# A spectral mixer with a token MLP: 256-column products with one weight tile paired into 512-column products

## The chip, the core and the metric

The kernel runs on one core of one Trainium2 chip, in one launch. The metric is the device time of that launch in microseconds. The matrix engine (TensorE, PE in the profile) multiplies tiles into PSUM, eight banks of 512 float32 columns by 128 partitions; VectorE (DVE) and ScalarE (ACT) read PSUM and work in SBUF; GpSimd (POOL) and SyncE (SP) mostly issue DMAs here. Each engine has its own queue of instructions, and semaphores order work between them.

## The reference

What matters of it (S = 2048 tokens, D = 512 channels, F = 1792 hidden units; all float32):

```python
x = A_x
xn = _layernorm(x, axis=-1)
# A: global filter
X = rfft2(xn) * (w_r + 1j * w_i)
s = irfft2(X)
# B: token mixing
h = _layernorm(xn)
u = gelu(einsum("bsd,sf->bdf", h, w1) + b1)
y = einsum("bdf,fs->bds", u, w2) + b2
g = silu(y.transpose(0, 2, 1))
return x + s * g
```

The change lies in the second product of B, here GEMM2: 2048 tokens by 512 channels, summed over 1792 hidden units.

## The kernel before, in words

Stages up to about 212 us: layer norms and GEMM1 with GELU, the spectral filter between them, and the forms of the hidden activations described below. The last stage is GEMM2 with the inverse channel transform and the output. Only it is touched.

**One step of Strassen's method (Winograd's form).** GEMM2 is cut into 2 x 2 blocks: output tokens (tile j0 = p and tile j1 = p + 8), hidden units (two halves of seven tiles of 128) and channels (left and right 256). Seven products of sums of blocks replace eight. Each product n has a weight form (seven 128 x 128 tiles, `w2_form`) and an activation form (seven tiles of 128 x 256, `forms`).

**High and low parts.** Each operand is split into a high part, rounded to a short mantissa, and a low remainder, and a product is three matrix products: high weight with high activation, high weight with low activation, low weight with high activation. A form tile holds the high part in its first 256 columns and the low part in the next 256, side by side (`high_low`, `form_parts`). For weights, ACT writes the high part (L706) and DVE the low part (L707).

**The loop.** `for p in range(NP)` runs over eight pairs of output tiles; inside, `ORDER = (1, 2, 5, 6, 3, 7, 4)` runs over the products. Each has 7 form tiles x 3 = 21 products of 256 columns (L828). They accumulate in the left halves of three banks: `bx` (bank 2 or 3, alternating with p) takes 1, then 6, 7 and 4 on top; `by` (bank 4) takes 2; `bz` (bank 5) takes 5, then 3 on top. As soon as a sum stands, ACT copies it out (`copied`, L790: p1, p5, v2), or DVE adds an earlier copy to it (`summed`, L798: c11, c12, c22), and ACT puts the result through SiLU (`gate`, L794). `finish` (L802) multiplies by the spectral result on DVE and a DMA on POOL's queue adds it to the output (L804), where x already lies.

**What else runs in a pair.** `channels` (L763) does the inverse channel transform of one output tile, and its DVE operations (L767 to L779) give y, which is split into ch (ACT) and cl (DVE, both L143); `spectral` (L146 to L148) then does three 512-column products, called the rotations below. DVE adds weight blocks for the forms 6 and 3 (L720, L726). SP's queue loads weight blocks (L695), and POOL's queue adds a second block in the DMA (L697). The weight forms are in three buffers (tag w2f) and are made two products ahead.

**What sets the order.** The code states the work of the stage in program order, and a scheduler places the instructions on each engine; each engine then runs its own in that order. So operations of one step can stand between those of another.

Of the kernel before, what the change touches and what calls it, by code (L numbers as in the profile page):

```python
# [8 lines left out]
F32 = mybir.dt.float32  # L9
# [6 lines left out]
P = 128  # L16
S, D, F = 2048, 512, 1792
# [3 lines left out]
NH = NF // 2  # L21
# [113 lines left out]
def spectral_mixer_kernel(tc, x, w1, b1, w2, b2, wk, we, wx, c_f, c_ft, c_d, c_i, c_g, c_h, out):  # L135
    nc = tc.nc
    V, A, G, T, SY = nc.vector, nc.scalar, nc.gpsimd, nc.tensor, nc.sync

    def pool(stack, side, name, bufs):
        return stack.enter_context(tc.tile_pool(name=name, bufs=bufs, side=side, reuse_waits="tile"))  # L140
# [9 lines left out]
    with tc.tile_pool(name="ps", bufs=1, space=PSUM) as psp, ExitStack() as left, ExitStack() as right:  # L150
        ps = psp.tile([P, 8, 512], F32, name="ps")
# [180 lines left out]

        def form_parts(n, i):
            t, k = form[i][n]
            return t[:, k, :D // 2], t[:, k, D // 2:]


        BATCHES = ((((4, 2), (10, 2)), (7, 2, 0, 1)), (((6, 1), (12, 2)), (7, 0, 1)))
# [45 lines left out]
        m = moments("m0", 2)  # L384
# [3 lines left out]
        m = {k: t[:, :1] for k, t in m.items()}  # L388
# [12 lines left out]
        c = turned(0, m, 0)  # L401
# [4 lines left out]
        m = moments("m2", 2)  # L406
        of.update({2: (m, 0), 3: (m, 1)})
        folds = iter(())
        for j in range(NJ):
            more = j + 1 < NJ  # L410
# [33 lines left out]
            if more:  # L444
# [7 lines left out]
                c = turned(j + 1, *of[j + 1])  # L452
# [4 lines left out]
            if more:  # L457
                low(w[1][1], raws[j + 1, 1], w[1][0])
                if FIRST <= j < FIRST + NE:
                    i = j - FIRST  # L460
# [5 lines left out]
                if j % 2 == 0 and j + 4 < NJ:  # L466
                    m = moments(f"m{j + 4}", 2)
# [23 lines left out]
        T = Kept(T, keep)  # L491
# [184 lines left out]
        for n in range(8):  # L676
            a, b, c, d, e, f = PACE[n]
# [69 lines left out]
        fp = pool(left, "left", "fin", 1)  # L747
# [6 lines left out]
        def gathered(j):  # L754
            yt = fp.tile([P, 4, P], F32, name=f"yt{j}", tag="yt", bufs=2)
            A.activation(yt.rearrange("p b (l c) -> p b l c", c=2), ey[:, :, :, j], AF.Copy)
            return yt

        def channels(j, yt):

            pe = ps[:, 6 + j // NP].rearrange("p (h b c) -> p h b c", b=2, c=P)
            for b in range(4):
                T.matmul(pe[:, b % 2, b // 2], yt[:, b], ci[:, b], start=True, stop=True)  # L763
# [15 lines left out]
            V.scalar_tensor_tensor(yv[:, 1, :, 1], t, -RT, ev[:, :, 1], op0=ALU.mult, op1=ALU.add)  # L779
            ch = fp.tile([P, D], F32R, name=f"ch{j}", tag="ch", bufs=2)  # L780
            cl = fp.tile([P, D], F32R, name=f"cl{j}", tag="cl", bufs=2)
            split(ch, cl, y)
            return ch, cl

        def spectral(j, y):
            mm3(ps[:, j // NP], cft[:, 0], cft[:, 1], *y, True, True)

        def copied(name, src):
            t = fp.tile([P, HD], F32, name=name, tag=name.split("_")[0])
            A.activation(t, src, AF.Copy)  # L790
            return t

        def gate(g, j, cols, src, scale):
            A.activation(g[:, cols], src, AF.Silu, bias=b2t[:, j:j + 1], scale=scale)  # L794

        def summed(name, a, b):
            t = fp.tile([P, HD], F32, name=name, tag="c", bufs=2)
            V.tensor_add(t, a, b)  # L798
            return t

        def finish(g, j, cols):
            V.tensor_mul(g[:, cols], ps[:, j // NP, cols], g[:, cols])  # L802
            if j + 1 < NJ:
                G.dma_start(out[:, j, cols], g[:, cols], accum_op=ALU.add)  # L804
            else:
                V.tensor_add(g[:, cols], g[:, cols], xr[:, cols])
                SY.dma_start(out[:, j, cols], g[:, cols])

        left_, right_, whole = slice(0, HD), slice(HD, D), slice(0, D)
        y0 = channels(0, gathered(0))  # L810
        for p in range(NP):
            j0, j1 = p, p + NP
            g0, g1 = (fp.tile([P, D], F32, name=f"g{j}", tag="g", bufs=2) for j in (j0, j1))
            bx, by, bz = ps[:, 2 + p % 2, :HD], ps[:, 4, :HD], ps[:, 5, :HD]
            for k, n in enumerate(ORDER):
                wf = ready.pop(0)
                w = next(wforms, None)
                if w is not None:
# [5 lines left out]
                o = {1: bx, 6: bx, 7: bx, 4: bx, 2: by, 5: bz, 3: bz}[n]  # L824
                for m, i in enumerate(FORMS):
                    uh, ul = form_parts(n, i)
                    for a, (wi, ui) in enumerate(((0, uh), (0, ul), (1, uh))):
                        T.matmul(o, wf[:, wi, i], ui, start=m + a == 0 and n in (1, 2, 5), stop=m == NH - 1 and a == 2,  # L828
                                 skip_group_check=n in (6, 3, 7, 4))
                if n == 1:  # L830
                    p1 = copied(f"p1_{p}", bx)
                    spectral(j0, y0)
                elif n == 5:
                    p5 = copied(f"p5_{p}", bz)
                elif n == 2:
                    gate(g0, j0, left_, summed(f"c11_{p}", by, p1), 1.0)
                elif n == 6:
                    v2 = copied(f"v2_{p}", bx)
                    y1 = channels(j1, yt)
                elif n == 3:  # L840
                    gate(g0, j0, right_, summed(f"c12_{p}", bz, v2), 1.0)
                    finish(g0, j0, whole)
                elif n == 7:
                    gate(g1, j1, right_, summed(f"c22_{p}", bx, p5), -1.0)
                    spectral(j1, y1)
                    if p + 1 < NP:
                        y0 = channels(j0 + 1, yt)
                    else:
                        finish(g1, j1, right_)
                else:  # L850
                    gate(g1, j1, left_, bx, -1.0)
                    finish(g1, j1, whole if p + 1 < NP else left_)


# [35 lines left out]
```

## Time and profile before

| | us |
|---|---|
| median of 3 runs | 391.57 (389.78 to 392.61) |
| the profiled execution | 387.47 |
| its span, first to last instruction | 385.7 |
| GEMM2 stage, from 212.2 to the end of the span | 173.5 |
| mean granted TensorE clock | 0.993 of full speed |

Rows of the profile read: engine, line, operation, output tile <- input tiles, shapes, count. In groups the numbers behind the bar are total busy us and mean ns of one, then idle time before it and what ended it; in a timeline the first two are start and length in us. An engine's operations overlap at their ends, so the distance from one start to the next is shorter than a row's length. The chain of waits follows the last instruction back to what released each step. PE's ends are modelled; its starts carry the pace.

### The profile page before, as it was taken

To read this page: it belongs to the slowest core of one execution; us is meant where nothing else is said; L and a number is where in the kernel's file an instruction comes from. 1 tells how busy PE (TensorE), PEld (TensorE's weight loads), DVE (VectorE), ACT (ScalarE), POOL (GpSimd) and SP (SyncE) were. 2 spreads that over 40 slices of the span, in tenths; PEclk is the share of its full clock that TensorE was granted. 3 is DMA by queue.
4 is the path that set the end of the run, shared out by engine and by line. 5 is a ranking of instruction groups with operands and counts; after the bars stand their busy time and mean duration, and the time that the engine had idled before them with its cause. 6 is when DMAs were issued, how large, how long until landed. Compare 5 with 4: busy or idle time off the path is not lost.

```text
span 385.7 us, 7939 instructions
## 1 busy us (share of the span) xinstructions
PE 374.0 (97%) x2872; PEld 328.8 (85%) x2872; DVE 323.2 (84%) x734; ACT 227.6 (59%) x412; POOL 78.6 (20%) x133
## 2 busy tenths in 40 slices
PE   7999999999999999999799989999999999999994
PEld 4888888888778878777588979999999999999994
DVE  5899999986579999897995999796979787887873
ACT  4677776764843455575417695565656564646541
POOL 2133233231302333233001003030202020210100
PEclk9999999999999999999899999999999999999999
DMA  8974777312636889988828398896979787885602
GB/s 262 300 251 155 266 254 241 97 55 82 198 77 173 211 226 256 245 226 193 259 71 253 57 274 208 214 215 166 201 153 214 140 230 143 220 165 156 98 0 55
DMA packets 39143, 70.01 MB, mean 182 GB/s; under 512 B 5424, under 2 KB 21440, under 8 KB 38976
## 3 DMA queue, kind: packets, MB, share of 16 engines
q1 hardware_dynamic: 30048, 48.14, 39.8%
q0 software_dynamic: 9056, 21.38, 29.3%
q8 instruction: 22, 0.36, 0.4%
q14 instruction: 17, 0.14, 0.1%
HBM read 61.10 MB, written 8.13 MB: 179 GB/s over the span
## 4 chain that ended last, share of the span: by engine, by line
PE 73%; DVE 9%; DMA 9%; issue 5%; ACT 1%; POOL 1%; SPq 0%; DVEq 0%; POOLq 0%; ACTq 0%
PE ps L828 28%; PE ps L377 20%; PE ps L132 16%; PE ps L241 4%; PE ps L763 3%; DMA s<-in_w_dram 2%; DMA out_dram<-g 2%; DVE w2f L707 2%; DMA w1l<-in_w_dram 2%; PE ps L366 1%; DMA w1s<-in_w_dram 1%; PE ps L147 1%; PE ps L148 1%; DMA hf<-in_c_h_dram 1%; DVE xc L589 1%
## 5 line engine op out<-in xcount | busy, mean ns | idle before, releaser
L377 PE MATMUL ps<-h,w1h 128*128 128x512 f32 x224 | 58.7, 398 | 0.0
L132 PE MATMUL ps<-h,w1h 128*128 128x512 f32 x152 | 49.6, 408 | 0.0
L707 DVE TENSOR_TENSOR w2f<-s,w2f 128x896 fp32r<-128x896 f32 x32 | 34.8, 1092 | 16.6 <-ACT w2f L706 15.8
L377 PEld LDWEIGHTS ps<-h,w1h 128*128 128x128 f32 x224 | 40.9, 188 | 7.9
L828 PE MATMUL ps<-fa,w2f 128*128 128x256 f32 x336 | 43.4, 282 | 0.0
L828 PE MATMUL ps<-fc,w2f 128*128 128x256 f32 x336 | 41.7, 280 | 1.0 <-DVE w2f L707 0.6
L828 PE MATMUL ps<-fb,w2f 128*128 128x256 f32 x336 | 42.5, 281 | 0.1
L828 PEld LDWEIGHTS ps<-fa,w2f 128*128 128x128 f32 x336 | 41.6, 188 | 0.8
L828 PEld LDWEIGHTS ps<-fc,w2f 128*128 128x128 f32 x336 | 40.3, 188 | 1.6 <-DVE w2f L707 0.8
L828 PEld LDWEIGHTS ps<-fb,w2f 128*128 128x128 f32 x336 | 40.4, 188 | 0.5 <-DVE c L798 0.5
L697 POOL DMA_DIRECT2D s<-in_w_dram x16 | 13.9, 870 | 122.0 <-DMA s<-in_w_dram 36.7
L706 ACT ACTIVATE w2f<-s 128x896 fp32r<-128x896 f32 x32 | 30.2, 949 | 14.1 <-DVE s L720 10.9
L132 PEld LDWEIGHTS ps<-h,w1h 128*128 128x128 f32 x152 | 27.7, 192 | 9.9 <-issue 4.9
L707 DVE TENSOR_TENSOR w2f<-a,w2f 128x896 fp32r<-128x896 f32 x24 | 26.0, 1085 | 9.5 <-ACT w2f L706 9.5
L132 PE MATMUL ps<-h,w1l 128*128 128x512 f32 x76 | 30.1, 396 | 2.8 <-DMA w1l<-in_w_dram 2.8
L377 PE MATMUL ps<-h,w1l 128*128 128x512 f32 x112 | 30.6, 389 | 0.0
L706 ACT ACTIVATE w2f<-a 128x896 fp32r<-128x896 f32 x24 | 22.8, 950 | 11.8 <-PE ps L828 7.3
L377 PEld LDWEIGHTS ps<-h,w1l 128*128 128x128 f32 x112 | 21.0, 188 | 4.5
L589 DVE SCALAR_TENSOR_TENSOR xc<-xc,turn,px 128x512 f32<-128x512 f32 x32 | 23.9, 747 | 0.2 <-issue 0.2
L372 DVE TENSOR_TENSOR w1l<-w1r,w1h 128x512 fp32r<-128x512 f32 (+1 forms) x32 | 20.9, 652 | 2.1 <-ACT w1h L369 1.9
L804 POOL DMA_DIRECT2D out_dram<-g x15 | 13.5, 902 | 43.8 <-DVE g L802 43.8
L794 ACT ACTIVATE g<-c,b2t 128x256 f32<-128x256 f32 x24 | 12.1, 505 | 15.9 <-DVE c L798 13.3
(128 smaller groups left out, 765.5 us busy)
## 6 DMA issues: line engine op xcount, KB each, us to landing
a<-in_w_dram SPq DMA_DIRECT2D x24, 448.0 KB, 4.0
wt<-in_wk_dram POOLq DMA_DIRECT2D x16, 512.0 KB, 4.7
s<-in_w_dram SPq DMA_DIRECT2D x16, 448.0 KB, 4.3
s<-in_w_dram POOLq DMA_DIRECT2D x16, 448.0 KB, 6.7
w1s<-in_w_dram SPq DMA_DIRECT2D x36, 128.0 KB, 3.2
w1r<-in_w_dram SPq DMA_DIRECT2D x16, 256.0 KB, 3.6
xc<-px SPq DMA_DIRECT2D x64, 64.0 KB, 4.1
x<-in_x_dram SPq DMA_DIRECT2D x15, 256.0 KB, 3.7
```

What stands on the lines that cost most here:

```text
L132: return lambda *args, **kw: self.keep(operation(*args, **kw))
L241: T.matmul(z[:, b], h[:, b * P:(b + 1) * P], c, start=True, stop=True)
L372: keep(V.tensor_sub(dst, src, hi.bitcast(F32)))
L377: T.matmul(ps[:, bank + i], w[wi][:, i * P:(i + 1) * P], hj, start=first and j == 0, stop=last and j == NJ - 1)
L589: V.scalar_tensor_tensor(to, zt, turn[:, k:k + 1], px[:, ::-1], op0=ALU.mult, op1=ALU.add)
L697: G.dma_start(t, w2_half(*added), accum_op=ALU.add)
L706: A.activation(wf[:, 0], v, AF.Copy)
L707: V.tensor_sub(wf[:, 1], v, wf[:, 0].bitcast(F32))
L763: T.matmul(pe[:, b % 2, b // 2], yt[:, b], ci[:, b], start=True, stop=True)
L794: A.activation(g[:, cols], src, AF.Silu, bias=b2t[:, j:j + 1], scale=scale)
L804: G.dma_start(out[:, j, cols], g[:, cols], accum_op=ALU.add)
L828: T.matmul(o, wf[:, wi, i], ui, start=m + a == 0 and n in (1, 2, 5), stop=m == NH - 1 and a == 2, skip_group_check=n in (6, 3, 7, 4))
```

## The change

A form tile's two parts lie side by side, so that the high weight tile can meet both in one product of 512 columns: `form_parts` also returns the whole tile. The left half of the bank then sums high x high and low x high, the right half high x low. In the pairs 0 to 6 (`wide`) each form tile has one product of 512 columns and one of 256; the last pair keeps three of 256. What is read from a bank is 512 columns wide, and the two halves are added on DVE: `copied` copies both halves, `summed` adds copy and bank over 512 columns and then the right half to the left, in place. For product 4, which was read straight from PSUM by the gate, the right half is copied by ACT and added by DVE. The copies now share one tag with two buffers, p5 has its own.

```diff
         def form_parts(n, i):
             t, k = form[i][n]
-            return t[:, k, :D // 2], t[:, k, D // 2:]
+            return t[:, k], t[:, k, :D // 2], t[:, k, D // 2:]
...
         def copied(name, src):
-            t = fp.tile([P, HD], F32, name=name, tag=name.split("_")[0])
+            n = src.shape[-1]
+            five = name[:2] == "p5"
+            t = fp.tile([P, D], F32, name=name, tag="p5" if five else "part", bufs=1 if five else 2)[:, :n]
             A.activation(t, src, AF.Copy)
             return t
...
-        def summed(name, a, b):
-            t = fp.tile([P, HD], F32, name=name, tag="c", bufs=2)
-            V.tensor_add(t, a, b)
-            return t
+        def summed(src, t):
+            V.tensor_add(t, src, t)
+            if t.shape[-1] > HD:
+                V.tensor_add(t[:, :HD], t[:, :HD], t[:, HD:])
+            return t[:, :HD]
...
-            bx, by, bz = ps[:, 2 + p % 2, :HD], ps[:, 4, :HD], ps[:, 5, :HD]
+            wide = p + 1 < NP
+            bx, by, bz = (ps[:, b, :D if wide else HD] for b in (2 + p % 2, 4, 5))
...
                 for m, i in enumerate(FORMS):
-                    uh, ul = form_parts(n, i)
-                    for a, (wi, ui) in enumerate(((0, uh), (0, ul), (1, uh))):
-                        T.matmul(o, wf[:, wi, i], ui, start=m + a == 0 and n in (1, 2, 5), stop=m == NH - 1 and a == 2,
-                                 skip_group_check=n in (6, 3, 7, 4))
+                    both, uh, ul = form_parts(n, i)
+                    if wide:
+                        T.matmul(o, wf[:, 0, i], both, start=m == 0 and fresh, stop=m == NH - 1, skip_group_check=True)
+                    else:
+                        T.matmul(o, wf[:, 0, i], uh, start=m == 0 and fresh, stop=False, skip_group_check=more)
+                        T.matmul(o, wf[:, 0, i], ul, start=False, stop=False, skip_group_check=more)
+                    T.matmul(o[:, :HD], wf[:, 1, i], uh, start=False, stop=m == NH - 1, skip_group_check=more or wide)
...
-                    gate(g1, j1, left_, bx, -1.0)
+                    gate(g1, j1, left_, summed(bx[:, :HD], copied(f"low_{p}", bx[:, HD:])) if wide else bx, -1.0)
```

Where the instructions stand now. On PE, in pair 4, between the products 5 and 6 (w2f5_4, w2f6_4 are the weight forms, fc the activation forms), before:

```order
L828 MATMUL ps_58<-fc5_2766,w2f5_4_3836 128x256 x3
L828 MATMUL ps_58<-fc6_2772,w2f5_4_3836 128x256 x3
L828 MATMUL ps_58<-fc2_1437,w2f6_4_3866 128x256 x3
L828 MATMUL ps_58<-fc1_1562,w2f6_4_3866 128x256 x3
L828 MATMUL ps_58<-fc0_2421,w2f6_4_3866 128x256 x3
```

and after:

```order
L833 MATMUL ps_58<-fc5_2766,w2f5_4_3652 128x512
L837 MATMUL ps_58<-fc5_2766,w2f5_4_3652 128x256
L833 MATMUL ps_58<-fc6_2772,w2f5_4_3652 128x512
L837 MATMUL ps_58<-fc6_2772,w2f5_4_3652 128x256
L833 MATMUL ps_58<-fc2_1437,w2f6_4_3675 128x512
L837 MATMUL ps_58<-fc2_1437,w2f6_4_3675 128x256
```

Three instructions of 256 columns per form tile have become one of 512 and one of 256; the order of the form tiles is the same.

On DVE, at the same place of pair 4, with the sum of product 2 (c11 before, p1 after), the weight additions (s1) and the low parts of the weight forms, before:

```order
L720 TENSOR_TENSOR s1_12_3613<-s1_12_3613,a12_4_3616 128x896
L707 TENSOR_TENSOR w2f6_4_3866<-s1_12_3613,w2f6_4_3866 128x896
L798 TENSOR_TENSOR c11_4_3897<-ps_58,p1_4_3860 128x256
L726 TENSOR_TENSOR s1_12_3613<-s1_12_3613,a11_4_3648 128x896
L707 TENSOR_TENSOR w2f3_4_3901<-s1_12_3613,w2f3_4_3901 128x896
L707 TENSOR_TENSOR w2f7_4_3929<-s4_4_3676,w2f7_4_3929 128x896
```

and after:

```order
L720 TENSOR_TENSOR s1_12_3468<-s1_12_3468,a12_4_3471 128x896
L799 TENSOR_TENSOR p1_4_3669<-ps_58,p1_4_3669 128x512
L801 TENSOR_TENSOR p1_4_3669<-p1_4_3669 128x256
L707 TENSOR_TENSOR w2f6_4_3675<-s1_12_3468,w2f6_4_3675 128x896
L726 TENSOR_TENSOR s1_12_3468<-s1_12_3468,a11_4_3496 128x896
L707 TENSOR_TENSOR w2f3_4_3703<-s1_12_3468,w2f3_4_3703 128x896
L707 TENSOR_TENSOR w2f7_4_3724<-s4_4_3517,w2f7_4_3724 128x896
```

The sum of product 2 has moved ahead of the low part of form 6, and the addition of the halves (L801) stands behind it.

On DVE, later in pair 4, around the sum of product 7 (p5) and the output tile g4, after:

```order
L801 TENSOR_TENSOR v2_4_3744<-v2_4_3744 128x256
L799 TENSOR_TENSOR p5_4_3722<-ps_58,p5_4_3722 128x512
L767 TENSOR_TENSOR es5_3822<-ps_58,od5_3820 128x256
L805 TENSOR_TENSOR g4_3650<-ps_58,g4_3650 128x512
L801 TENSOR_TENSOR p5_4_3722<-p5_4_3722 128x256
L768 TENSOR_TENSOR es5_3822<-ps_58,od5_3820 128x256
L707 TENSOR_TENSOR w2f2_5_3837<-a11_5_3706,w2f2_5_3837 128x896
```

Before, the multiplication (L802) of that tile came first, then the sum of product 7, then the low part of form 2 and both halves of es. Now the halves of v2 stand ahead of the sum of product 7, and the multiplication, whose gate needs them, two operations behind.

On PE, from the end of product 7 to product 4 of pair 4, after:

```order
L837 MATMUL ps_58<-fb6_2771,w2f7_4_3724 128x256
L146 MATMUL ps_58<-ch12_3763,cft_63 128x512
L763 MATMUL ps_58<-cd_64,yt5_3772 128x128 x4
L833 MATMUL ps_58<-fd2_1366,w2f1_5_3793 128x512
L147 MATMUL ps_58<-cl12_3764,cft_63 128x512
L148 MATMUL ps_58<-ch12_3763,cft_63 128x512
L837 MATMUL ps_58<-fd2_1366,w2f1_5_3793 128x256
L833 MATMUL ps_58<-fd2_1366,w2f1_5_3793 128x512
L837 MATMUL ps_58<-fd2_1366,w2f1_5_3793 128x256
L833 MATMUL ps_58<-fb2_1436,w2f4_4_3767 128x512
```

Before, only the rotations (L146 to L148) and the four products of L763 stood between the products 7 and 4, and product 1 of the next pair followed product 4. Now two couples of that product 1 (w2f1_5) stand ahead of product 4 as well.

More of the change, by code (lines that the diff above doesn't have):

```diff
@@ L824, in spectral_mixer_kernel @@
                 o = {1: bx, 6: bx, 7: bx, 4: bx, 2: by, 5: bz, 3: bz}[n]
+                fresh, more = n in (1, 2, 5), n in (6, 3, 7, 4)
                 for m, i in enumerate(FORMS):
-                    uh, ul = form_parts(n, i)
-                    for a, (wi, ui) in enumerate(((0, uh), (0, ul), (1, uh))):
-                        T.matmul(o, wf[:, wi, i], ui, start=m + a == 0 and n in (1, 2, 5), stop=m == NH - 1 and a == 2,
-                                 skip_group_check=n in (6, 3, 7, 4))
+                    both, uh, ul = form_parts(n, i)
[5 more added lines that the diff above has]
+                    T.matmul(o[:, :HD], wf[:, 1, i], uh, start=False, stop=m == NH - 1, skip_group_check=more or wide)
                 if n == 1:
@@ L835, in spectral_mixer_kernel @@
                 elif n == 2:
-                    gate(g0, j0, left_, summed(f"c11_{p}", by, p1), 1.0)
+                    gate(g0, j0, left_, summed(by, p1), 1.0)
                 elif n == 6:
@@ L840, in spectral_mixer_kernel @@
                 elif n == 3:
-                    gate(g0, j0, right_, summed(f"c12_{p}", bz, v2), 1.0)
+                    gate(g0, j0, right_, summed(bz, v2), 1.0)
                     finish(g0, j0, whole)
                 elif n == 7:
-                    gate(g1, j1, right_, summed(f"c22_{p}", bx, p5), -1.0)
+                    gate(g1, j1, right_, summed(bx, p5), -1.0)
                     spectral(j1, y1)
```

## The prediction

> **What bounds the kernel now.** I read the page first: busy time, then the chain of work that ended last.
>
> ```profile
> PE 374.0 (97%) x2872; PEld 328.8 (85%) x2872; DVE 323.2 (84%) x734; ACT 227.6 (59%) x412; POOL 78.6 (20%) x133
> PE 73%; DVE 9%; DMA 9%; issue 5%; ACT 1%; POOL 1%; SPq 0%; DVEq 0%; POOLq 0%; ACTq 0%
> PE ps L828 28%; PE ps L377 20%; PE ps L132 16%; PE ps L241 4%; PE ps L763 3%; DMA s<-in_w_dram 2%; DMA out_dram<-g 2%; DVE w2f L707 2%; DMA w1l<-in_w_dram 2%; PE ps L366 1%; DMA w1s<-in_w_dram 1%; PE ps L147 1%; PE ps L148 1%; DMA hf<-in_c_h_dram 1%; DVE xc L589 1%
> ```
>
> TensorE (PE) holds the chain, and the changed line, L828, is its largest single part, 28% of the span. Since L828 runs only in the last stage (212 us to the end), I asked for that chain in order of time, and for the busy time of two whole pairs (one round of the loop over p).
>
> ```profile
> 302.11 7.42 PE ps L828 x63
> 322.63 7.42 PE ps L828 x63
> 343.34 7.42 PE ps L828 x63
> ...
> 302.11:322.63 20.52, 20.52 (x172) 20.12 (x171) 16.73 (x33) 12.20 (x20) 3.47 (x4) 1.00 0.81 183
> 322.63:343.34 20.71, 20.71 (x171) 20.30 (x171) 16.90 (x33) 12.18 (x20) 3.47 (x4) 1.00 0.82 181
> ```
>
> A pair lasts (343.34 - 302.11) / 2 = 20.62 us. The windows give length and then busy time of PE, its weight loads, VectorE (DVE), ScalarE (ACT), GpSimd: PE is busy through both, DVE for 16.8 us, ACT for 12.2, at the full granted clock. So in a settled pair PE sets the pace, and DVE has 3.8 us to spare. Where that lies is in DVE's timeline (in brackets: idle time before, and what ended it):
>
> ```profile
> 322.59 1.09 DVE L720 TENSOR_TENSOR s<-s,a 128x896 f32<-128x896 f32 x1
> 324.76 1.09 DVE L707 TENSOR_TENSOR w2f<-s,w2f 128x896 fp32r<-128x896 f32 x1 [1.08 <-ACT w2f L706]
> 325.77 0.42 DVE L798 TENSOR_TENSOR c<-ps,p 128x256 f32<-128x256 f32 x1
> 326.10 1.08 DVE L726 TENSOR_TENSOR s<-s,a 128x896 f32<-128x896 f32 x1
> 328.28 2.21 DVE L707 TENSOR_TENSOR w2f<-s,w2f 128x896 fp32r<-128x896 f32 x2 [1.10 <-ACT w2f L706]
> 331.34 1.09 DVE L707 TENSOR_TENSOR w2f<-a,w2f 128x896 fp32r<-128x896 f32 x1 [0.85 <-ACT w2f L706]
> 340.72 0.69 DVE L802 TENSOR_TENSOR g<-ps,g 128x512 f32<-128x512 f32 x1 [0.55 <-ACT g L794]
> ```
>
> Two holes, 1.08 and 1.10 us, are a relay: DVE adds a weight form (L720, L726), ACT rounds its high part, DVE takes the low part (L707). They don't shrink when PE is faster. The other two, 0.85 and 0.55, come from ACT operations that had themselves waited for PE, and give way.
>
> The first two pairs look otherwise:
>
> ```profile
> 215.00:220.00 5.00, 4.93 (x42) 4.72 (x41) 5.00 (x12) 3.39 (x7) 0.00 (x0) 1.00 0.01 2
> 220.00:225.00 5.00, 4.09 (x34) 3.69 (x33) 4.32 (x9) 4.22 (x8) 0.00 (x0) 1.00 0.75 247
> 225.00:230.00 5.00, 4.37 (x35) 4.05 (x34) 4.90 (x12) 5.00 (x9) 0.87 (x1) 1.00 0.89 229
> 230.00:235.00 5.00, 5.00 (x42) 4.86 (x41) 5.00 (x14) 3.43 (x6) 0.31 (x1) 1.00 0.90 307
> ...
> 222.20 0.51 PE L828 MATMUL ps<-fc,w2f 128*128 128x256 f32 x2 [0.29 <-ACT w2f L706]
> 223.33 2.50 PE L828 MATMUL ps<-fc,w2f 128*128 128x256 f32 x19 [0.62 <-DVE w2f L707]
> 227.61 0.50 PE L146 MATMUL ps<-ch,cft 128*128 128x512 f32 x1 [0.63 <-ACT ch L143]
> ```
>
> From 215 to 235 us DVE is busy 19.2 of 20, and PE waits for DVE and ACT: there PE is not the bound.
>
> **The change, part by part.** *The products.* A couple of 256-column products with one weight tile becomes a 512-column one. What each costs is its distance to the next start in a dense stretch:
>
> ```profile
> 204.69 0.40 PE L146 MATMUL ps<-h,w1h 128*128 128x512 f32 x1
> ...
> 211.97 0.39 PE L148 MATMUL ps<-h,w1l 128*128 128x512 f32 x1
> 212.20 2.63 PE L828 MATMUL ps<-fd,w2f 128*128 128x256 f32 x21
> ...
> 304.42 5.11 PE L828 MATMUL ps<-fc,w2f 128*128 128x256 f32 x42
> 309.37 1.05 PE L763 MATMUL ps<-cd,yt 128*128 128x128 f32 x8
> 310.18 2.72 PE L828 MATMUL ps<-fa,w2f 128*128 128x256 f32 x21
> ```
>
> From 204.69 to 212.20 there are 33 products of 512 columns: 7.51 / 33 = 0.2276 us. Between 304.42 and 309.37 there are 42 of 256: 4.95 / 42 = 0.1179 us. A merge therefore saves 2 x 0.1179 - 0.2276 = 8.2 ns: nearly all of the time is the columns, whose number stays. There are 7 products x 7 forms = 49 merges in a pair and 7 wide pairs (the last stays narrow), 343 in all: 0.40 us a pair, 2.8 us together. That is all that PE can give, and 0.7% of the run.
>
> The Trainium skill ("TensorE: Matmul & The Clock Gate", section "Back-to-back issue gap") has N/2.4 + 2.5 ns for a warm product. By it the couple costs 218.3 ns and the wide one 215.8, the saving would be 2.5 ns each and 0.9 us in all; the trace's 235.8 and 227.6 are both larger and further apart, and the measurement decides.
>
> *DVE.* These rows (groups by line, shapes kept apart; the second number is ns of one) price what is added:
>
> ```profile
> L802 DVE TENSOR_TENSOR g<-ps,g 128x512 f32<-128x512 f32 x15 | 10.3, 687 | 3.8 <-ACT g L794 3.8
> L798 DVE TENSOR_TENSOR c<-ps,p 128x256 f32<-128x256 f32 x16 | 6.7, 416 | 0.7 <-PE ps L828 0.7
> L806 DVE TENSOR_TENSOR g<-g,xr 128x256 f32<-128x256 f32 x1 | 0.4, 425 | 0.0
> L143 ACT ACTIVATE ch<-y 128x512 fp32r<-128x512 f32 x16 | 10.0, 627 | 3.1 <-DVE y L779 3.1
> L790 ACT ACTIVATE p<-ps 128x256 f32<-128x256 f32 x15 | 5.6, 374 | 3.6 <-PE ps L828 3.6
> ```
>
> Three sums in a wide pair read 512 columns of PSUM and not 256: 3 x (0.687 - 0.416) = 0.81 us. Each then adds its halves, 256 columns in SBUF like L806: 3 x 0.425 = 1.28. The fourth, for form 4, is new: 0.42. By durations 2.5 us. But neighbours overlap: L798 starts at 325.77 and the next at 326.10, so a 256-column operation takes 0.33 of the engine, and by that the sum is 0.8 + 4 x 0.33 = 2.1. I take 2.3 a pair.
>
> Does it fit? The order shows that the first relay hole (1.08) now holds the two operations of the form-2 sum: 0.6 + 0.33 of work. The second hole (1.10) stays empty. DVE then needs 16.8 + 2.3 + 1.1 = 20.2 us a pair; PE needs 20.62 - 0.40 = 20.22. That is a tie. Within the pair the tight place is the form-2 sum, which now stands ahead of form 6's low part in DVE's queue and waits for the last form-2 product. After that product DVE needs 0.69 + 0.43 + 1.09 = 2.2 us until the low part is there. PE does form 5 meanwhile, 7 x (0.2276 + 0.1179) = 2.42, and one wide product of form 6, so it asks after 2.6 us: 0.4 to spare. Behind the waiting sum stand form 6's low part, L726 and through ACT form 3. I expect the tie to give back a quarter of the gain: 0.3 us a pair kept (from 0.4 with no stall to nothing), over the five settled pairs (p from 2 to 6) 1.5 us.
>
> Between forms 7 and 4 PE must wait until the form-7 sum has left the bank both share. That read grows by 0.27 us, and stands later in DVE's queue, behind the v2 halves. In the new order two couples of the next pair's form 1 (0.69 us) stand as filler ahead of form 4, with the three rotations (0.68) and the channel products (8 x 0.11 = 0.89): about 2.2 us of cover. I cost it at nothing as long as DVE reaches the sum within 1.5 us of form 7's end (2.2 less the read's 0.69); beyond that each pair pays the excess.
>
> *ACT.* Three copies of 512 instead of 256 columns and one new: 3 x (0.627 - 0.374) + 0.374 = 1.1 us, 13.3 of 20.2 busy. It hides, but lengthens the hops in which DVE waits for ACT; this is in the quarter above.
>
> *The first two pairs.* DVE is the bound, so the 0.8 us that PE could save isn't realised. In pair 0 the new work is the same 2.3 us; ahead of form 6 a DVE hole takes part of it, later the filler does. The first output's DMA decides the second pair:
>
> ```profile
> 221.08 0.42 DVE L798 TENSOR_TENSOR c<-ps,p 128x256 f32<-128x256 f32 x1
> 222.18 1.09 DVE L707 TENSOR_TENSOR w2f<-s,w2f 128x896 fp32r<-128x896 f32 x1 [0.68 <-ACT w2f L706]
> 233.47 0.69 DVE L802 TENSOR_TENSOR g<-ps,g 128x512 f32<-128x512 f32 x1
> 236.22 1.22 POOL L804 DMA_DIRECT2D out_dram<-g  x1
> 245.23 0.51 ACT L794 ACTIVATE g<-c,b2t 128x256 f32<-128x256 f32 x1 [2.65 <-DMA out_dram<-g]
> 253.84 0.50 PE L147 MATMUL ps<-cl,cft 128*128 128x512 f32 x1 [0.38 <-DVE cl L143]
> ```
>
> A gate waits 2.65 us for that DMA, and PE feels 0.38 of it later. The output was ready at 234.16 and issued at 236.22, behind two weight loads on POOL's queue: 2.1 us of slack. The new work ahead of it on DVE is 0.27 + 0.43 + 0.27 + 0.43 + 0.27 = 1.7, less 0.68 for the hole: 1.0. It still fits. For the two pairs I take +0.3 us, the middle between a gain of 0.4 and a loss of 1.0.
>
> **The sum.** -1.5 + 0.3 = -1.2 us. The profiled execution took 387.47 us (385.7 of span and 1.8 around it), so it becomes 386.3. The median of the three runs, 391.57, lies 4.1 above it; the same difference there gives 390.4.
>
> **Rivals.** *DVE becomes the bound (slower).* A waiting DVE operation holds up what stands behind it. The gate on ACT now waits for one more DVE operation, the addition of the halves, and the multiplication L805 on DVE waits for the gate: a new relay. Before, only one of the two multiplications of a pair had such a hole (0.55). In the new order of pair 4 only two other operations, 0.6 + 0.33 us, stand between the v2 halves and the multiplication that needs their gate (0.5 us on ACT, behind other work there). If both multiplications wait 0.55 us, DVE needs 16.8 + 2.3 + 1.1 + 1.1 = 21.3 us a pair, 0.7 more than now; with 0.5 for the first pairs that is 7 x 0.7 + 0.5 = 5.4 us: 397.0. It decides from 0.4 us of new holes a pair (20.2 against 20.62). For it: the tie. Against: in pair 3 a form and a low part stand between, 1.6 us, enough for the gate. 0.18, of which 0.12 above 1%.
>
> *Nothing changes.* The couple of 512 and 256 columns costs what three products of 256 did (0.354 us), or the tie eats all: 391.6. No row has the two sizes alternate, but the step from L148 into 212.20 shows no loss. 0.16.
>
> *Weight loads set the pace of short products (faster).* The eight 128-column products from 309.37 to 310.18 take 0.81 / 8 = 0.10 us each, hardly under the 0.118 of twice the columns: a floor per instruction, perhaps its weight load. With a wide product ahead to hide the load, a 256-column one could fall to its columns alone: (0.2276 - 0.1179) / 256 = 0.43 ns a column, 0.110 us, 8 ns less. That is 343 x 8 ns = 2.8 us more; with the full 2.8 of the merges 386.0. Against: the 512-column products, which hide their loads, have the same fixed 8 ns. 0.06. The Trainium skill (same page, section "LDWEIGHTS (loading the stationary operand)") puts a load of 128 columns at 107 ns; by that it fits under a 256-column product already, and this rival gains nothing. No row here separates the two.
>
> **The numbers.** Forecast 0.60, its own range 388.8 (all of 2.8) to 391.6. The range reaches up into the slower rival and leaves out its upper part (0.12) and the faster rival (0.06): 387.4 to 395.0. The runs shown spread over 0.7%, so about 1%, 3.9 us, is what can be told from no change. Faster by more: 0.06, the last rival. Slower by more: 0.12. Within: 0.82.
>
> **What would show it.** Right: the profile after has couples 0.345 us apart, pairs of 20.2 to 20.4 us, DVE above 18.8 us of them, its hole ahead of form 6 gone, PE without waits above 0.3 us in pairs 2 to 6, and pairs 0 and 1 no shorter than before. Wrong: PE waits for DVE (a low part of form 6 or 3, or the bank ahead of form 4) in each settled pair, or couples other than 0.345.

## The result and the profile after

The changed kernel takes 391.4 us (389.38 to 393.39, 22 runs) beside 391.16 us for the kernel before (388.8 to 392.61, 22 runs) on the same chip: ratio 1.0007, 95% interval 0.9988 to 1.0026. A second series of the same kernel gave 389.65 us and 0.9975 (0.9945 to 1.0005). It is no different within what can be measured.

The first part of the page after and its chain of waits:

```profile
PE 375.6 (97%) x2529; PEld 313.5 (81%) x2529; DVE 336.6 (87%) x762; ACT 233.0 (60%) x419; POOL 78.5 (20%) x133
...
PE 92%; DVE 3%; DMA 2%; ACT 2%; issue 1%; POOL 0%; DVEq 0%; POOLq 0%
```

PE lost the 343 instructions that were merged (2872 to 2529), but not the time: its busy time is no smaller. DVE has 13 us more. The profiled execution took 390.63 us with a span of 388.9, 3.2 us above the profile before. That does not come from GEMM2: PE's timeline ahead of it, where the instructions are the same, shows a longer wait for a weight load of GEMM1, and GEMM2's stage starts later. Before (first line, and 212.20) and after:

```profile
187.46 0.47 PE L132 MATMUL ps<-h,w1l 128*128 128x512 f32 x1 [2.58 <-DMA w1l<-in_w_dram]
...
190.75 0.77 PE L132 MATMUL ps<-h,w1l 128*128 128x512 f32 x1 [4.65 <-DMA w1l<-in_w_dram]
...
215.60 0.39 PE L833 MATMUL ps<-fd,w2f 128*128 128x512 f32 x1
```

TensorE's granted clock was lower there too: 0.77 on average from 185 to 200 us, before 0.89. In the second series' profile the stage starts at 213.08, so the same kernel alone differs by 2.5 us there. So I compare the **stage**: from the first product of GEMM2 to the end of the span. Before it is 385.71 - 212.20 = 173.51 us, after 388.86 - 215.60 = 173.25 (from the unrounded times), in the second series 173.14.

Two whole pairs after, in the same view as before (length, then busy time of PE, its weight loads, DVE, ACT, GpSimd):

```profile
286.87:307.40 20.53, 20.53 (x122) 17.99 (x121) 18.54 (x37) 12.95 (x21) 3.25 (x5) 1.00 0.78 183
307.40:328.01 20.61, 20.61 (x122) 17.97 (x121) 18.87 (x37) 13.36 (x22) 3.98 (x5) 1.00 0.77 182
```

These two pairs take (328.01 - 286.87) / 2 = 20.57 us each, where two took 20.62; all five settled pairs together are 0.44 us longer than before (table below). PE is still busy throughout. So its products themselves take as long as before, and the start times in a dense stretch of form 5 and form 2 say so:

```profile
287.23 0.39 PE L833 MATMUL ps<-fc,w2f 128*128 128x512 f32 x1
287.46 0.28 PE L837 MATMUL ps<-fc,w2f 128*128 128x256 f32 x1
287.57 0.40 PE L833 MATMUL ps<-fc,w2f 128*128 128x512 f32 x1
287.81 0.28 PE L837 MATMUL ps<-fc,w2f 128*128 128x256 f32 x1
287.93 0.40 PE L833 MATMUL ps<-fc,w2f 128*128 128x512 f32 x1
...
291.47 0.39 PE L833 MATMUL ps<-fc,w2f 128*128 128x512 f32 x1
```

From 287.23 to 291.47 there are 12 couples: 4.24 / 12 = 0.3533 us each. Three 256-column products took 0.354. The merge gives nothing in these steps.

The holes of DVE in this pair:

```profile
287.14 0.69 DVE L799 TENSOR_TENSOR p<-ps,p 128x512 f32<-128x512 f32 x1
287.87 0.42 DVE L801 TENSOR_TENSOR p<-p 128x256 f32<-128x256 f32 x1
288.21 1.08 DVE L707 TENSOR_TENSOR w2f<-s,w2f 128x896 fp32r<-128x896 f32 x1
...
291.44 2.10 DVE L707 TENSOR_TENSOR w2f<-s,w2f 128x896 fp32r<-128x896 f32 x2 [1.02 <-ACT w2f L706]
...
303.69 0.42 DVE L799 TENSOR_TENSOR low<-ps,low 128x256 f32<-128x256 f32 x1 [0.35 <-ACT low L792]
304.53 1.09 DVE L707 TENSOR_TENSOR w2f<-s,w2f 128x896 fp32r<-128x896 f32 x1 [0.41 <-ACT w2f L706]
```

The relay hole ahead of form 6's low part (288.21) is filled by the sum of product 2 (L799, L801), as the prediction said, and the second (1.02) stayed. Two small ones are new.

### How the stage is taken apart

For every kernel below I took the distance from each w2f product's start to the next one's start in the trace, and the mean of those that no wait lengthens (up to 8% over their median). The number of products (343 wide and 490 narrow after, 1176 narrow before) times these means is "products"; "rest" is the stage less that: rotations, channel products, waits, the end. "First two" is from the stage's start to pair 2's first form-5 product, "five pairs" from there to pair 7's. Times in us, steps in ns. The profiles come from several chips.

| kernel | stage | wide, narrow step | couple | products | rest | first two | five pairs |
|---|---|---|---|---|---|---|---|
| before | 173.51 | -, 117.4 | 3 x 117.4 = 352.1 | 138.0 | 35.5 | 50.99 | 103.17 |
| after | 173.25 | 232.7, 118.7 | 351.4 | 138.0 | 35.3 | 50.24 | 103.61 |
| r_after | 173.14 | 232.8, 118.8 | 351.6 | 138.1 | 35.1 | 50.22 | 103.67 |
| e1_grouped | 171.22 | 230.1, 117.0 | 347.2 | 136.3 | 34.9 | 50.02 | 102.18 |
| r_e1_grouped | 173.44 | 230.1, 117.1 | 347.2 | 136.3 | 37.1 | 51.85 | 102.18 |
| e2_unmerged | 174.65 | -, 117.2 | 351.7 | 137.9 | 36.8 | 51.47 | 103.94 |
| e3_left_only | 172.56 | 232.5, 118.2 | 350.6 | 137.6 | 34.9 | 51.55 | 102.08 |
| e5_twos | 171.14 | 230.4, 117.5 | 347.9 | 136.6 | 34.5 | 49.75 | 102.36 |
| r_e5_twos | 171.09 | 230.5, 117.4 | 347.9 | 136.6 | 34.5 | 49.67 | 102.43 |
| e7_all_wide | 206.48 | 229.2, 115.8 | - | 174.3 | 32.2 | 60.78 | 126.69 |
| e8_pool_halves | 184.03 | 230.1, 116.0 | 346.1 | 135.8 | 48.3 | 56.66 | 108.44 |
| e9_grouped_left | 169.96 | 229.9, 116.0 | 346.0 | 135.7 | 34.2 | 49.87 | 101.15 |
| e10_shifted | 171.63 | 232.0, 118.1 | 350.1 | 137.5 | 34.2 | 49.77 | 102.92 |
| e11_before_twos | 172.53 | -, 117.1 | 351.4 | 137.7 | 34.8 | 50.33 | 103.18 |

The narrow mean takes in the last pair, which is all narrow products. Within the wide pairs alone the couple is 351.8 after, 351.9 in e3_left_only, 346.8 in e1_grouped, 346.1 in e9_grouped_left, 347.7 in e5_twos and 351.0 in e10_shifted; so the differences of e3_left_only to after in the table come from the last pair.

Kernels that ran twice agree in the five pairs within 0.07 us. The first two pairs are less steady: r_e1_grouped is 2.2 us longer than e1_grouped, 1.8 of it there, where PE waited for the first forms out of the stage ahead:

```profile
219.70 0.50 PE L833 MATMUL ps<-fa,w2f 128*128 128x512 f32 x1 [0.94 <-DVE fa L302]
...
223.85 0.50 PE L833 MATMUL ps<-fc,w2f 128*128 128x512 f32 x1 [1.04 <-DVE fc L302]
```

### The profile page after: what moved, and what is told of

Read it like the earlier page. It is cut to its first block, busy times and chain, and to the rows that moved or that the text cites. A ratio compares the mean times of both kernels' runs of the same rounds, so it can differ in the third digit from the quotient of the medians.

```text
span 388.9 us, 7289 instructions
## 1 busy us (share of the span) xinstructions
PE 375.6 (97%) x2529; PEld 313.5 (81%) x2529; DVE 336.6 (87%) x762; ACT 233.0 (60%) x419; POOL 78.5 (20%) x133
## 4 chain that ended last, share of the span: by engine, by line
PE 92%; DVE 3%; DMA 2%; ACT 2%; issue 1%; POOL 0%; DVEq 0%; POOLq 0%
PE ps L132 26%; PE ps L377 20%; PE ps L833 19%; PE ps L837 11%; PE ps L241 4%; PE ps L763 3%; PE ps L146 2%; DMA w1l<-in_w_dram 2%; PE ps L366 2%; PE ps L835 2%; PE ps L836 1%; PE ps L147 1%; PE ps L148 1%; DVE w2f L707 1%; ACT w2f L706 0%
## 5 line engine op out<-in xcount | busy, mean ns | idle before, releaser
L707 DVE TENSOR_TENSOR w2f<-s,w2f 128x896 fp32r<-128x896 f32 x32 | 34.2, 1088 | 9.7 <-ACT w2f L706 9.7
L706 ACT ACTIVATE w2f<-s 128x896 fp32r<-128x896 f32 x32 | 29.6, 947 | 17.2 <-DVE s L720 15.1
L833 PE MATMUL ps<-fc,w2f 128*128 128x512 f32 x98 | 35.3, 397 | 1.2 <-ACT w2f L706 1.1
L833 PE MATMUL ps<-fa,w2f 128*128 128x512 f32 x98 | 36.2, 400 | 0.0
L833 PE MATMUL ps<-fb,w2f 128*128 128x512 f32 x98 | 35.1, 395 | 0.0
L837 PE MATMUL ps<-fc,w2f 128*128 128x256 f32 x112 | 31.8, 284 | 0.0
L837 PE MATMUL ps<-fa,w2f 128*128 128x256 f32 x112 | 31.7, 283 | 0.1
L837 PE MATMUL ps<-fb,w2f 128*128 128x256 f32 x112 | 31.5, 281 | 0.0
L833 PEld LDWEIGHTS ps<-fc,w2f 128*128 128x128 f32 x98 | 18.4, 188 | 5.8 <-ACT w2f L706 1.3
```

The source lines that it names most:

```text
L706: A.activation(wf[:, 0], v, AF.Copy)
L707: V.tensor_sub(wf[:, 1], v, wf[:, 0].bitcast(F32))
L833: T.matmul(o, wf[:, 0, i], both, start=m == 0 and fresh, stop=m == NH - 1, skip_group_check=True)
L837: T.matmul(o[:, :HD], wf[:, 1, i], uh, start=False, stop=m == NH - 1, skip_group_check=more or wide)
```

## The experiments

**The same kernel again** (r_after).

> The changed kernel again, for the spread of the last stage's length (first product of GEMM2 to the end of the span; 173.3 us in the first profile of it, 173.5 before the change). If the 3.4 us by which the stage began later in the first profile came from chance, the stage begins within 1 us of 212.2 or anywhere between 210 and 217 here, and the stage itself lasts 172.9 to 173.7.

It came out as the first time, 173.14 us and the same steps (table). Of each edit below, only the lines that matter are shown.

**Is it the order of sizes, the width, or the reading?** Three kernels. e1_grouped runs the seven wide products of a weight form first, then the seven narrow ones:

```
+                if wide:
+                    for m, i in enumerate(FORMS):
+                        uh = form_parts(n, i)[1]
+                        T.matmul(o[:, :HD], wf[:, 1, i], uh, start=False, stop=m == NH - 1, skip_group_check=True)
```

> In the wide pairs all seven 512-column products of a form come first, then the seven of 256. Theory A (sizes that alternate cost the gain: 233 + 119 ns a couple and not 228 + 118): 512-column starts come 228 ns apart and 256-column ones 118, a product of 7 + 7 takes 2.42 us and not 2.46, the stage shrinks by up to 343 x 6 ns = 2.1 us to about 171.2. Theory B (512-column products are slower in this stage whatever stands between them, by the other traffic in it): 512-column starts stay 232 to 234 ns apart and the stage is within 0.6 us of 173.3.

e2_unmerged keeps all the new reading and undoes the merge: three narrow products, the one with the low form going to the right half of the bank:

```
+                    to = o[:, HD:] if wide else o
+                    T.matmul(o[:, :HD], wf[:, 0, i], uh, start=m == 0 and fresh, stop=False, skip_group_check=more or wide)
+                    T.matmul(to, wf[:, 0, i], ul, start=False, stop=wide and m == NH - 1, skip_group_check=more or wide)
```

> Three products of 256 columns per form tile as before the change, but high x low goes to the right half of the bank, so that all the new reading and adding stays. If the products' gain is as small as the starts say (353 against 352 ns for a form tile) the stage takes 173.3 + 343 x 1 to 2 ns = 173.6 to 174.0 us; if the merge is worth what was predicted (8 ns) it takes 176. Against the kernel before it shows what the new DVE and ACT work costs alone: 0 to 0.5 us if it hides, 1.5 to 3 us if DVE is the bound.

e3_left_only keeps the merge and reads only the left halves, as before the change. This leaves the product of high weight and low form out of the result:

```
-            bx, by, bz = (ps[:, b, :D if wide else HD] for b in (2 + p % 2, 4, 5))
+            bx, by, bz = (ps[:, b, :HD] for b in (2 + p % 2, 4, 5))
...
-                    gate(g1, j1, left_, summed(bx[:, :HD], copied(f"low_{p}", bx[:, HD:])) if wide else bx, -1.0)
+                    gate(g1, j1, left_, bx, -1.0)
```

> The merged products, but only the left half of each bank is read, copied and added, as before the change; the product of high weight and low activation in the right half is left out of the result. If the new DVE and ACT work holds PE up (about 1.5 us of waits by the first profile), the stage shrinks by that, to about 171.8 us; if that work hides, the stage stays within 0.4 us of 173.3.

e1_grouped: 388.41 us, ratio to before 0.9967 (0.9934 to 1.0000). In its timeline the products stand in runs:

```profile
285.63 1.77 PE L833 MATMUL ps<-fc,w2f 128*128 128x512 f32 x7
287.24 0.99 PE L841 MATMUL ps<-fc,w2f 128*128 128x256 f32 x7
288.06 1.77 PE L833 MATMUL ps<-fc,w2f 128*128 128x512 f32 x7
...
293.01 0.96 PE L841 MATMUL ps<-fa,w2f 128*128 128x256 f32 x7
293.80 1.76 PE L833 MATMUL ps<-fb,w2f 128*128 128x512 f32 x7
```

Seven wide products take 287.24 - 285.63 = 1.61 us, 0.230 each; seven narrow ones 0.82, 0.117 each. The couple is 0.347, where the alternating order has 0.3533 in the stretch shown. So the size of the steps depends on the order. (The run at 293.01 shows narrow products at 0.79 / 7 = 0.113: more on that at the end.) e2_unmerged: 391.3 us, 1.0018 (0.9986 to 1.005): undoing the merge under the new reading makes the stage 174.65 - 173.25 = 1.4 us longer, all of it in "rest", and most of it in the unsteady first two pairs (51.47 against 50.24); in the five pairs it is 0.3. The stage is longer than the 173.6 to 174.0 that I expected of a small gain, but the steps don't tell the merged products from the unmerged. e3_left_only: 388.16 us, 0.9944 (0.9911 to 0.9976), but its steps don't move (351.9 within the wide pairs): the reading isn't what holds the couples. Its stage, 172.56, lies between my two expectations, because two effects oppose each other: the five pairs are 1.5 us shorter than after (102.08 against 103.61), the first two 1.3 us longer. So the new work does cost time in settled pairs.

**What about the order?** e5_twos has two wide, then two narrow products, and so on:

```
+                        if m % 2 or m == NH - 1:
+                            for q in range(m - m % 2, m + 1):
+                                k_ = FORMS[q]
+                                T.matmul(o[:, :HD], wf[:, 1, k_], form_parts(n, k_)[1], start=False, stop=q == NH - 1, skip_group_check=True)
```

> Products in groups of two: two of 512 columns, then the two of 256 columns with the low parts, and so on; so in a product of seven weight tiles the size changes 8 times and not 14. Stage = first product of GEMM2 to the end of the span (after 173.25 and 173.14 us, fully grouped 171.22). If each change of size has a price (4.4 ns a couple in the alternating order, 351.8 against 347.4 ns), the mean couple is 349.6 ns here and the stage about 172.2 to 172.4 us. If something other than the change of size made the grouped kernel faster, as the sixth and seventh low parts coming later than the waits ahead of a form, the stage is 171.2 to 171.5 with the steps of a couple at 347 already, or stays at 173.2 with steps of 351.8.

e7_all_wide lets the low weight tile meet both parts too, which adds the low-by-low product to the sum:

```
-                    T.matmul(o[:, :HD], wf[:, 1, i], uh, start=False, stop=m == NH - 1, skip_group_check=more or wide)
+                    T.matmul(o, wf[:, 1, i], both if wide else uh, start=False, stop=m == NH - 1, skip_group_check=more or wide)
```

> The low weight tile meets both parts too, so every product of a wide pair has 512 columns; it adds the low-by-low product, which the sum left out so far. 343 products grow by some 0.113 us: about 39 us longer, so 429 us. Weight tiles still alternate between high and low as in after. If the change of size is what cost the gain, 512-to-512 steps are 230 ns or less; if it is the alternation of high and low tiles, they are 233 ns or more. If dense reading of PSUM by VectorE and ScalarE is what holds a 512-column product at 230 here and 227.6 ahead of the stage, the steps fall below 229, since the same reading is spread over a longer time.

e10_shifted holds each narrow product back by one wide product of the next form, so sizes alternate but neighbours differ in tile and data:

```
+                    if wide:
+                        for q in (m - 1,) * (m > 0) + (m,) * (m == NH - 1):
+                            k_ = FORMS[q]
+                            T.matmul(o[:, :HD], wf[:, 1, k_], form_parts(n, k_)[1], start=False, stop=q == NH - 1, skip_group_check=True)
```

> The low product of each weight tile follows one wide product later (wide 0, wide 1, low 0, wide 2, low 1, ..., wide 6, low 5, low 6): sizes still alternate at nearly every step, but neighbours differ in weight tile, form and data. If the alternation of sizes itself holds the steps, they stay near 232.6 and 119 ns (couple 351 to 352), the stage at 172.5 to 173.2 us, a little below after since the low parts may come later. If it is that the short product follows the wide one with the same weight tile's form and the same data, the couple falls to 346 to 348 ns and the stage to 171 to 171.5, as in groups of two and of seven.

e5_twos: 388.08 us, 0.9947 (0.9918 to 0.9977). The theory of a price for each change of size falls: eight changes instead of fourteen should have left 349.6 ns, and it has 347.9; its steps from wide to narrow are 230.2 and from narrow to wide 116.9, as cheap as those between equals. e7_all_wide: 422.73 us, 1.0824 (1.0749 to 1.0898), with high and low tiles in turn, at a pace the rows show:

```profile
298.37 0.39 PE L833 MATMUL ps<-fa,w2f 128*128 128x512 f32 x1
298.60 0.39 PE L837 MATMUL ps<-fa,w2f 128*128 128x512 f32 x1
...
300.66 0.39 PE L833 MATMUL ps<-fa,w2f 128*128 128x512 f32 x1
```

From 298.37 to 300.66 there are ten: 0.229 each. So changing the weight tile at each product, with the same data twice in a row, isn't the cause either. The stage grew by 33.2 us and not 39: "products" grew by 36.3 and not 39, as steps of one size are shorter than alternating ones, and "rest" fell by 3. e10_shifted: 388.41 us, 0.9969 (0.9942 to 0.9996). Its steps where the size changes are 231.9 and 119.0, a couple of 350.9: the expectation for alternation itself, 351 to 352, is nearly met, with other neighbours than in the changed kernel. Its stage is below what I expected (171.63, not 172.5 to 173.2), and that is "rest": 34.2.

What follows: strict alternation of the two widths costs about 4 to 5 ns a couple against groups of two or of seven, and neither the weight tile, the data, the reading nor the number of changes does. (In groups, the reading has a small part: 346.8 with it, 346.1 without.) What in the chip makes it so no run shows.

**How much does the new work on DVE and ACT hold back?** e9_grouped_left joins e1_grouped and e3_left_only: seven and seven, only left halves read, the product of high weight and low form left out of the result. e8_pool_halves has the products of e1_grouped and moves the addition of the halves to GpSimd:

```
-                V.tensor_add(t[:, :HD], t[:, :HD], t[:, HD:])
+                G.tensor_add(t[:, :HD], t[:, :HD], t[:, HD:])
```

> Grouped products, and only the left halves are read: this leaves the product of high weight with low form out of the result. It takes all of the new work off VectorE and ScalarE. If that work still costs the grouped kernel what it cost the alternating one (stage 173.25 to 172.56, 0.6 to 0.7 us), the stage is 170.5 us; if it hides, 171.2. Steps of a couple: 347.4 ns if reading PSUM has no part in them, 345 or less if the denser reading slows the 512-column products.

> Grouped products as before in the study, and the two halves of each sum are added on GpSimd instead of VectorE, 28 additions of 256 columns, which GpSimd's rows of this size put at roughly 1 us each. If VectorE's new work still costs the grouped kernel time, the stage falls from 171.22 to 170.6 or less. If it hides there already, it stays at 171.1 to 171.4. If the longer hop from sum to gate or GpSimd's queue of transfers delays the gates and the two relays, it is 172 or longer and the waits of TensorE grow.

e9_grouped_left: 386.59 us, 0.9887 (0.9838 to 0.9935). Two of its pairs:

```profile
285.03:305.25 20.22, 20.22 (x123) 17.87 (x122) 16.71 (x32) 12.15 (x21) 3.47 (x4) 1.00 0.78 186
305.25:325.49 20.24, 20.24 (x123) 17.87 (x122) 16.71 (x32) 12.16 (x21) 3.47 (x4) 1.00 0.79 185
```

Here PE alone sets the pace: 20.23 us. With the reading (e1_grouped) the five pairs take 102.18 instead of 101.15, so the new work costs (102.18 - 101.15) / 5 = 0.2 us a pair when PE's products are fast. In the stage that is 171.22 - 169.96 = 1.3 us, where I had expected 0.6 to 0.7. In the alternating order it costs more, (103.61 - 102.08) / 5 = 0.3 a pair (after against e3_left_only), and without the merge (103.94 - 103.17) / 5 = 0.15 (e2_unmerged against before). Against before, more than waits differs. By the starts in the traces, the rotations and channel products of the five pairs take 16.1 us before and 15.1 in e3_left_only, which merges but has no new work; that is nearly all of the 1.1 us by which its five pairs are shorter. PE's order there is another: between L146 and L147 stand two channel products before, in e3_left_only four and a form product.

e8_pool_halves was slower: 401.15 us, 1.0271 (1.0225 to 1.0316). Its largest group of operations on GpSimd (busy, mean ns of one, idle before):

```profile
L801 POOL TENSOR_TENSOR p<-p 128x256 f32<-128x256 f32 x14 | 16.1, 1154 | 20.9 <-DVE p L799 20.8
```

And its list of waits in the stage (us in total, times, longest):

```profile
ACT g L796 <- POOL p L801: 14.8, 9, 2.7
...
DVE g L805 <- ACT g L796: 14.2, 8, 4.8
ACT ch L143 <- DVE y L779: 12.9, 12, 2.8
...
PEld ps L146 <- ACT ch L143: 9.4, 7, 4.4
```

An addition that took DVE 0.42 us takes GpSimd 1.15, the gate on ACT waits for it, DVE's multiplication waits for the gate, and what DVE does behind it (the rotations' input y) reaches PE late. That is the chain of the rival "DVE becomes the bound", one hop longer. In this profile the granted clock also falls to half for 3.4 us, at 248.5 us, so up to 1.7 us of the stage are not the waits'.

**Does the order alone do it?** e11_before_twos is the kernel before, nothing merged, with its narrow products in the order of the groups of two:

```
+                    T.matmul(o, wf[:, 0, i], uh, start=m == 0 and n in (1, 2, 5), stop=False, skip_group_check=n in (6, 3, 7, 4))
+                    T.matmul(o, wf[:, 0, i], ul, start=False, stop=False, skip_group_check=n in (6, 3, 7, 4))
+                    for q in (m,) if p + 1 == NP else range(m - m % 2, m + 1) if m % 2 or m == NH - 1 else ():
```

> The kernel before, with nothing merged and no new reading; only the order of its 256-column products changes to that of the groups of two: four products with two high tiles, then two with the low tiles. Five settled pairs took 103.17 us before, 102.36 and 102.43 in groups of two with merged products; the whole stage 173.51, 171.14 and 171.09. If the gain of the groups of two comes from the merge (wide steps of 230.4 instead of 2 x 117.4), this kernel stays at 103.1 to 103.3 and 173.2 to 173.6 us, with steps of 117.4 ns. If it comes from the order alone, because low tiles are asked for later and TensorE waits less, it falls to 102.4 to 102.7 and to 171.5 to 172.5 us with the same steps.

389.7 us, 1.0019 (0.9989 to 1.0048). The five pairs take 103.18 us, before 103.17: there the order alone gives nothing, and the 0.8 us that the groups of two are faster belong to the merge in that order. In the stage it is 1.0 us shorter than before, of which 0.7 in the first two pairs; r_e1_grouped shows that one run's start can differ by more than that, so this part isn't settled.

**The two better orders again.**

> Groups of two again, to settle the size of its gain: stage 171.1 us within 0.15, as in its first run, 2.4 us below the kernel before; ratio to before 0.994 (2.4 of 390), between 0.992 and 0.997. If its first ratio (0.9947) was luck of the stages ahead of GEMM2, it is nearer to 1 while the stage stays.

> Groups of seven again: stage 171.2 us within 0.15 and steps 230.3 and 117.1 ns; ratio to before 0.994 (2.3 us of 390), between 0.992 and 0.997, the same as groups of two.

r_e5_twos: 388.47 us, 0.9955 (0.9929 to 0.9981); stage 171.09. r_e1_grouped: 389.11 us, 0.997 (0.9941 to 0.9998); the expected stage was missed in its profile (173.44, the waits shown above), its steps were not. Of the kernels with the whole result, groups of two beat the kernel before by most, about 0.5% in both series, groups of seven and e10_shifted by about 0.3%, hardly clear of noise; the changed kernel was not measurably faster in either of its own.

## Why the prediction was right, and where it wasn't

The time was right, 390.4 forecast and 391.4 measured, "within 1%" at 0.82. But a range of 1% to both sides holds no change at all, so this says little about the mechanism. The forecast gain of 1.2 us was not right: the stage shows 0.3 (173.51 less 173.25 and 173.14). Of the signs that the prediction named, pairs of 20.2 to 20.4 us didn't come, and "couples other than 0.345", a sign of being wrong, did.

*The step that failed* is the first term of the sum: "A merge therefore saves 2 x 0.1179 - 0.2276 = 8.2 ns". It measured (352.1 - 351.4) = 0.7 ns, or 0.3 within the wide pairs, and products 138.0 us before and after where 2.8 less was to come. Two things were wrong in it. The 0.2276 was taken where 512-column products follow each other, ahead of the stage; within the stage even e1_grouped and e7_all_wide have 230 and 229, which makes a merge worth some 5 ns (352.1 - 347.2). The alternation took that: 351.4 against 347.2, x 343 = 1.4 us. Both sizes were read from rows of one size alone, and I added them as if a step knew nothing of its neighbour. The one row I set against the doubt, the step from L148 into 212.20, was a single change of size; e5_twos shows that single changes are indeed free.

*The rival "Nothing changes"*, with the couple at 0.354, is what happened (0.3533 in the stretch shown); it deserved more than 0.16, since no row spoke on the point that decided. The Trainium skill's rule for warm products ("TensorE: Matmul & The Clock Gate", section "Back-to-back issue gap"), by which 0.9 us were to be gained, comes nearer to the total than my rows did, but not to the steps, which are 6 to 9% above its N/2.4 + 2.5 ns and depend on the order.

*DVE.* 2.3 us of new work a pair: measured by the windows, 18.54 and 18.87 against 16.73 and 16.90, 1.9. The forecast "above 18.8" holds for one of the two. The hole ahead of form 6 went, the second stayed, as said.

*The tie.* Kept 0.3 of 0.4 us a pair, because waits would eat a quarter. The five pairs lost 103.61 - 103.17 = 0.44 us, 0.09 a pair, with products that gained nothing. That looks like the 0.1 that I gave the waits, but by luck: against e3_left_only, which has the same alternating products and the same steps, the new work costs 0.3 a pair, three times as much, and in groups 0.2 (e1_grouped against e9_grouped_left). The 0.2 a pair that e3_left_only gains over before, around the rotations, hid it. Some 0.9 of the 1.5 us of five pairs are the first rotation (L146), from whose start to the next it is 0.32 us on average after and 0.23 in e3_left_only. And 20.22 as PE's need, 20.62 - 0.40, is what e9_grouped_left reaches, but not by merges that save 8 ns: its steps give 49 x 6 ns = 0.3 of the 0.4, the order around the rotations the rest.

*Product 4's bank.* I costed the wait between forms 7 and 4 at nothing, and PE's timeline has no wait there in the settled pairs. What waits there, weight loads in the list of waits from 262 to 372 us, is small:

```profile
PEld ps L146 <- ACT ch L143: 1.1, 5, 0.3
PEld ps L837 <- DVE w2f L707: 0.3, 1, 0.3
```

*ACT.* It was to hide and lengthen hops: this list shows the rotations waiting for ACT's high part five times (before: not once), the relay through which the new copies are felt; without the new work (e3_left_only) the list is empty.

*The first two pairs.* +0.3 forecast, -0.75 measured (50.99 to 50.24). Pair 0 has six channel products more in it (0.67 us) and pair 1 six fewer, so pair 0 stayed and pair 1 gained. Before, pair 1 lost some 0.7 us on PE (by the starts of its products in the trace) when a gate waited 2.65 us for the first output's DMA; I asked only whether the new work makes that output late. But it delays the gate as well: besides the kernel before, the three without the new reading, e3_left_only, e9_grouped_left and e11_before_twos, wait 3.1, 2.1 and 2.4 us there, those with it and the additions on DVE 0 to 1.6. The new work stands where the wait was. That this made the 0.75 isn't shown: e11_before_twos has the wait and none of the new work, and takes 50.33.

*DVE becomes the bound* didn't come, but e8_pool_halves shows its chain at work once the addition takes 1.15 us. *Weight loads set the pace of short products* fell: with a wide product ahead, a narrow one takes 118.7 ns, not less, and runs at 113 occur without a wide one ahead (below). So the condition it named isn't what brings 0.110. The floor that it read from the channel products, 0.10 us each, is a mean too: by the starts in the trace they are 108 to 112 ns apart, and only the last is 31 ns ahead of the product behind it.

## What to carry to other kernels

A price read from products of one size is not the price in a mixed order: when a change makes sizes alternate, put them in groups of two or more, or look for a row with the mix. Merging matmuls that share weights saved at most some 5 ns each here (352.1 to 346.8), so it must not add work to an engine that is nearly the bound (DVE, 18.7 of 20.6 us with the new work): in groups of seven that work ate 1.3 of some 3.5 us (e1_grouped's stage against e9_grouped_left's and before's). When the spans of two profiles differ by more than the effect, compare from the first changed instruction on.

## What the hardware showed that I had not expected

Steps of TensorE fall into fixed patterns that hold for long stretches, at full granted clock and without waits. In the stretch shown after, starts in the trace are 237, 118, 231, 118, 233, 123 ns apart, over and over: 1060 ns for three couples. Elsewhere in the same kernel the couple is 349. Equal wide products repeat 226, 229, 232; ahead of the stage 227, 227, 226. Runs of narrow products hold either 113 or 118 ns, as the two narrow runs of e1_grouped show (0.79 and 0.82 us for seven), and the kernel before has mostly 118. The share of the fast pattern is larger where less is read from PSUM (mean 116.0 in e9_grouped_left, 117.0 in e1_grouped), but in one kernel, products that start beside a DVE or ACT operation on PSUM differ from the others by less than 2 ns, either way. What picks the pattern stays open.
